# Layer ends in column form with weights as the stationary operand, and the second layer's end done once for all four batches

## The chip, the cores and the metric

The kernel runs on one core of a Trainium2 chip. The metric is device time in microseconds (us) of one execution. Executions of one kernel spread by 1 to 2% here, so medians and intervals are given; profiles are single executions. A run is called slow when it is over 1.5% above the fastest of its kernel in the same rounds, and fast otherwise; ratios use fast runs alone. Engines: PE multiplies matrices (PEld is its weight load), DVE is VectorE, ACT is ScalarE, POOL is GpSimd, SP issues the DMAs.

## The reference, cut to what matters

```
# A: attention block, B: gated block; 4 batches, one token each, D=512
# 32 query heads, 8 K/V heads, 4096 positions of 128; F=1792
x = x + A(layernorm(x))      # q = x@wq, softmax(q k^T / sqrt(128)) v, then @ wo
x = x + B(layernorm(x))      # (sigmoid(x@w_gate) * (x@w_up)) @ w_down
x = x + A(layernorm(x))      # the same weights and the same K/V cache
x = x + B(layernorm(x))
```

Below, "layer 1" and "layer 2" are the two passes through A and B. The "end" of a layer is everything after the attention values: output projection with `wo`, residual, layernorm, gate, up, down, residual. K is read once (both layers use it while it is in memory); V is read twice.

## The kernel before

The program keeps a list of operations with names of what they read and write; a small scheduler, working with assumed durations, fixes the order of each engine in advance. A PSUM bank is one name, so two operations that use one bank are ordered by the program's text, whatever their priority. K and V come through a ring of 22 slots of 512 KB. K tiles hold 16 slots from their load until layer 2's scores of that batch.

The ends of both layers are in row form: activations are the stationary operand (one column), weights stream past as the moving operand, and four matmuls work on four column groups of 32.

```
    def y_proj(s, oi, prio, gis=range(4)):            # output projection
        for gi in gis:
            for h in range(16 * s + gi * R, 16 * s + gi * R + R):
                for j in range(4):
                    mm(G_ps[32*j:32*j+1, 0:P], oT[oi][:, h:h+1], wo[:, h, j*P:(j+1)*P], h == 0, h == H-1)
            S.put("pe", ..., writes=["G"])
    def glu(x, xkey, o, okey, prio, last):
        layer_norm(x, xkey, xT[:], "xT", prio, True)   # rows; a matmul turns them into columns
        # gate into G_ps, up into U_ps: 16 matmuls each, 448 moving columns
        # tanh and multiply on 128x448, 5 small matmuls to columns, copy, 56 matmuls for down into G_ps
    ...
    for b in range(B):
        ...                                            # values and y_proj of layer 1
        cross(0, b, 0, PX)                             # end of layer 1, priority 0 (first)
        ...                                            # q projection and scores of layer 2
        if b > 0:
            for s in range(NH):
                y_proj(s, 1, PC)                       # end of layer 2 of the batch before,
            cross(1, b - 1, 1, PC)                     # priority 4 (last)
```

Of the kernel before, what the change touches and what calls it, by code (L numbers as in the profile page):

```python
# [12 lines left out]
RATE = 0.419  # L13
# [184 lines left out]
def bass_interleave_layers__gqa_block_cached__glu_gated_glu__decode_kernel(nc, A_x, A_k, A_v, A_wq, A_wo, B_x, B_wg, B_wu, B_wd, out):  # L198
# [3 lines left out]
    R = H // G  # L202
# [33 lines left out]
    wd = sb("wd", [P, 4, 3, D], bf)  # L236
    wd_r = sb("wd_r", [P, 2, D], bf)

    xin = [sb(f"xin{b}", [P, P], bf) for b in range(B)]
    xs = [sb(f"xs{i}", [P, P]) for i in range(2)]  # L240
    xc = sb("xc", [P, P], bf)
    cols = sb("cols", [P, 32])
    xsum = cols[:, 0:2]
    nmean, vpe, mhalf, rs_h = (cols[:, i:i + 1] for i in range(2, 6))
    rs_q = [[cols[:, 6 + 4 * l + b:7 + 4 * l + b] for b in range(B)] for l in range(2)]
    rows, nrows, ones, nbias = (cols[:, i:i + 1] for i in range(14, 18))
    ls = cols[:, 18:20]
    nM = cols[:, 20:20 + R]
    xT = sb("xT", [P, KD], bf)
    xT1 = sb("xT1", [P, KD, B], bf)  # L250
# [7 lines left out]
    th = sb("th", [P, FS])  # L258
    junk = th[:, FS - P:FS]
    h_sb = th[:, 0:FS // 2].bitcast(bf)  # L260
    hT = sb("hT", [P, 14], bf)
    oT = [sb(f"oT{i}", [P, H], bf) for i in range(2)]
# [17 lines left out]
    U_ps = ps("U_ps", [P, 512])  # L280

    sel4 = ident_b[:].rearrange("p (j y) -> p j y", y=32)[:, :, 0]
# [9 lines left out]
    sem_names += [f"wo{i}" for i in range(4)] + ["wg", "wu", "wd", "wd_r0", "wd_r1"]  # L292
    sem_names += [f"x{b}" for b in range(B)] + [f"out{b}" for b in range(B)]
# [11 lines left out]
    for name, t in (("ident_b", ident_b), ("rows", rows), ("nrows", nrows), ("mask_a", mask_a), ("sel_den", sel_den)):  # L305
        S.put("pool", lambda e, t=t: e.memset(t[:], 0.0), 0.15, 0, writes=[name])
    S.put("pool", lambda e: e.memset(mhalf[:], -0.5), 0.1, 0, writes=["mhalf"])
    S.put("pool", lambda e: e.memset(ones[:], 1.0), 0.1, 0, writes=["ones"])
    S.put("pool", affine(ident_b, ident_b[:], [[-1, P]], 0, 1.0), 0.3, 0, reads=["ident_b"], writes=["ident_b"])
    for j in range(4):  # L310
        S.put("pool", affine(rows, rows[:], [[0, 1]], -32 * j, 1.0 / D), 0.2, 0, reads=["rows"], writes=["rows"])
        S.put("pool", affine(nrows, nrows[:], [[0, 1]], -32 * j, -1.0 / D), 0.2, 0, reads=["nrows"], writes=["nrows"])
# [6 lines left out]
    for b in range(B):  # L319
        S.put("dve", lambda e, b=b: e.memset(xin[b][:], 0.0), 0.1, 0, writes=[f"xin{b}"])  # L320
    for b in range(B):
        S.put(
            "act", lambda e, b=b: e.dma_start(
                xin[b][bass.ds(0, 4, step=32), :], A_x[b, 0, :].rearrange("(j p) -> j p", j=4)
            ), 0.3, 0, writes=[f"xin{b}"], dma=f"x{b}",
        )
    for name, t, v in (("ml", ml, 1.0), ("mt", mt, 0.0), ("S0", S_ps[0], 0.0), ("S1", S_ps[1], 0.0), ("S2", S_ps[2], 0.0), ("G", G_ps, 0.0), ("U", U_ps, 0.0)):
        S.put("dve", lambda e, t=t, v=v: e.memset(t[:], v), 0.4, 0, writes=[name])
# [39 lines left out]
    def load_wd():  # L368
        src = B_wd.rearrange("(j f) n -> j f n", j=4)
        load_w(  # L370
            "wd", wd[:].rearrange("p j c n -> p j (c n)"),
            src[:, 0:FM, :].rearrange("j (p c) n -> p j (c n)", c=3), P * 12 * D * 2,
        )
        for i in range(2):
            load_w(
                f"wd_r{i}", wd_r[i * FR:(i + 1) * FR],
                src[2 * i:2 * i + 2, FM:FS, :].rearrange("j p n -> p j n"), FR * 2 * D * 2,
            )
# [30 lines left out]
    def stat(bank, key, c, src, si, w, wkey, prio):  # L409
        S.put(  # L410
            "pe", mm(bank[:, c:c + 1], col(w), xsum[:, si:si + 1]), 0.4, prio,
            reads=[f"xsum{si}", wkey], writes=[key],
        )

    def layer_norm(x, xkey, xT_ap, xT_key, prio, summed):
        if not summed:
            S.put(
                "dve", lambda e: e.tensor_scalar(junk, x[:], 1.0, None, op0=ALU.mult, op1=ALU.add, accum_out=xsum[:, 0:1]),  # L418
                0.35, prio, reads=[xkey], writes=["th", "xsum0"],
            )  # L420
        stat(U_ps, "U", 448, xsum, 0, nrows, "nrows", prio)
        S.put(
            "dve", lambda e: e.tensor_scalar(xc[:], x[:], U_ps[:, 448:449], None, op0=ALU.add), 0.3, prio,
            reads=[xkey, "U"], writes=["xc"],
        )
        S.put("dve", lambda e: e.tensor_copy(nmean[:], U_ps[:, 448:449]), 0.15, prio, reads=["U"], writes=["nmean"])  # L426
        S.put(
            "act", lambda e: e.activation(junk, x[:], ACTF.Square, bias=nmean[:], accum_out=xsum[:, 1:2]), 0.6, prio,  # L428
            reads=[xkey, "nmean"], writes=["th", "xsum1"],
        )  # L430
        S.put("pe", mm(U_ps[:, 452:456], xc[:], sel4), 0.25, prio, reads=["xc", "ident_b"], writes=["U"])
        S.put("dve", lambda e: e.tensor_copy(xT_ap, U_ps[:, 452:456]), 0.18, prio, reads=["U"], writes=[xT_key])  # L432

    def rstd(mult, rs, rs_key, prio, bank, key, c):
        stat(bank, key, c, xsum, 1, rows, "rows", prio)
        S.put(
            "dve", lambda e: e.tensor_scalar(vpe[:], bank[:, c:c + 1], mult, mult * eps, op0=ALU.mult, op1=ALU.add),  # L437
            0.17, prio, reads=[key], writes=["vpe"],
        )
        S.put(  # L440
            "pool", lambda e: e.tensor_tensor(rs[:], vpe[:], mhalf[:], ALU.pow), 0.6, prio,  # L441
            reads=["vpe", "mhalf"], writes=[rs_key],
        )

    def q_proj(s, xT_of, n, dst, dkey, prio, xkey):
# [8 lines left out]
        S.put("pe", fns, 2.4, prio, reads=[xkey, f"wq{2 * s}", f"wq{2 * s + 1}"], writes=["M"])  # L454
# [27 lines left out]
    def scores(b, s, u, prio):  # L482
        for q in range(2):
            fns = []
            bank, bkey = S_ps[(2 * u + q) % 3], f"S{(2 * u + q) % 3}"
            for nn in range(NQ):
# [11 lines left out]
                "pe", fns, 1.6, prio, reads=[f"qbd{u % NQB}"] + [f"kT{b}{4 * s + gi}{q}" for gi in range(4)],  # L498
# [3 lines left out]
    def softmax(u, rs, rs_key, prio):  # L502
# [3 lines left out]
        for q in range(2):  # L506
# [10 lines left out]
            "dve", lambda e: e.tensor_reduce(nM[:], tr[:, 0:16].rearrange("p (a h) -> p h a", h=R), AX.X, ALU.min),  # L517
# [4 lines left out]
                mt[:, 0:16].rearrange("p (a h) -> p a h", h=R), nM[:].unsqueeze(1).broadcast_to([P, 4, R])  # L522
# [4 lines left out]
            "dve", lambda e: e.tensor_scalar(nbias[:], nb[:, 0:1], rs[:], None, op0=ALU.mult), 0.22, prio,  # L527
            reads=["tr", rs_key], writes=["nbias"],
        )
        for q in range(2):  # L530
# [3 lines left out]
                    bias=nbias[:], scale=rs[:], accum_out=ls[:, q:q + 1],  # L534
                ), 0.85, prio, reads=[f"S{banks[q]}", "nbias", rs_key], writes=[f"p_sb{q}", f"ls{q}"],
# [18 lines left out]
        i0 = ls[:].unsqueeze(2).broadcast_to([P, 2, 16])  # L554
# [13 lines left out]
    def values(l, b, s, pi, oi, prio, gis=range(4)):  # L568
        for gi in gis:
            for q in range(2):  # L570
# [9 lines left out]
                S.put("pe", fns, 0.62, prio, reads=[f"pt{pi}"], writes=["O"], tiles=[tile])  # L580
        c0, c1 = gis[0] * R, (gis[-1] + 1) * R
        S.put(
            "dve", lambda e: e.tensor_tensor(  # L583
                oT[oi][:, 16 * s + c0:16 * s + c1], O_ps[:, c0:c1], winv[pi][:, c0:c1], ALU.mult
            ), 0.2, prio - 1.5, reads=["O", f"winv{pi}"], writes=[f"oT{oi}{s}{gi}" for gi in gis],
        )

    def y_proj(s, oi, prio, gis=range(4)):
        for gi in gis:
            fns = []  # L590
            for h in range(16 * s + gi * R, 16 * s + gi * R + R):
                for j in range(4):
                    fns.append(mm(
                        G_ps[32 * j:32 * j + 1, 0:P], oT[oi][:, h:h + 1], wo[:, h, j * P:(j + 1) * P], h == 0, h == H - 1,
                    ))
            S.put("pe", fns, 0.5, prio, reads=[f"oT{oi}{s}{gi}", f"wo{2 * s + gi // 2}"], writes=["G"])

    def glu(x, xkey, o, okey, prio, last):
        layer_norm(x, xkey, xT[:], "xT", prio, True)
        for w, key, bank, bkey in ((wg, "wg", G_ps, "G"), (wu, "wu", U_ps, "U")):  # L600
            fns = []
            for k in range(KD):
                for j in range(4):
                    fns.append(mm(
                        bank[32 * j:32 * j + 1, 0:FS], xT[:, k:k + 1], w[:, k, j * FS:(j + 1) * FS], k == 0, k == KD - 1,
                    ))
            S.put("pe", fns, 1.1, prio, reads=["xT", key], writes=[bkey])
            if w is wg:
                rstd(4.0, rs_h, "rs_h", prio, G_ps, "G", 448)
        S.put(  # L610
# [92 lines left out]
    for b in range(B):  # L703
        if b > 0:
            values(1, b - 1, 0, pis[1, b - 1, 0], 1, PV, range(pre))
# [70 lines left out]
```

## Time and profile before

The median was 368.5 us. The profiled execution has a span of 369.9 us.

| what | value |
|---|---|
| read from HBM | 114.6 MB |
| PE, PEld, DVE busy | 69%, 49%, 41% |
| unhindered DMA | about 410 GB/s, so some 280 us for the bytes |

From the page of the kernel before: busy time of the engines, then the span in 40 slices (a digit is the busy share in tenths) and the rate of the DMA in GB/s by slice.

```profile
PE 255.4 (69%) x5752; PEld 180.1 (49%) x5752; DVE 152.2 (41%) x396; ACT 61.2 (17%) x147; POOL 14.2 (4%) x56
DMA  8999999997599999972999979854999989727800
GB/s 276 400 397 410 399 350 401 407 340 291 174 410 409 408 364 332 357 287 73 328 411 408 396 267 357 284 220 152 384 400 410 364 282 359 288 105 240 334 4 3
```

The holes (174, 73, 152, 105 GB/s) are where the ring is full and the queue waits; each comes at the change from layer 1 to layer 2 of a batch. The last 20 us move nothing.

By stages, cut where the q projection of layer 2 begins in each batch (88.8, 164.6, 243.6 and 324.2 us). Columns: stretch, its length, busy time of each engine with the number of instructions, granted clock of PE (the share of its full clock that it was given), DMA share, GB/s.

```profile
0.00:88.80 88.80, 42.15 (x793) 29.45 (x794) 33.96 (x90) 10.97 (x28) 8.17 (x45) 0.69 1.02 377
88.80:164.60 75.80, 54.80 (x1245) 38.53 (x1243) 34.32 (x81) 13.27 (x31) 1.09 (x2) 0.55 0.90 339
164.60:243.60 79.00, 60.74 (x1407) 42.96 (x1405) 36.28 (x90) 14.40 (x34) 1.64 (x3) 0.56 0.84 311
243.60:324.20 80.60, 61.82 (x1408) 43.18 (x1406) 36.22 (x90) 14.40 (x34) 1.64 (x3) 0.54 0.84 317
```

The second and third period contain a whole layer-2 end of the batch before, the first only half of a projection. In all three the DMA share is well under 1.

Single steps, from the timeline (start, duration, engine and operation, number of instructions, and in brackets the idle time before and what ended it; "issue" means that the profile shows nothing that the engine waited for). Most lines between these are left out:

```profile
19.23 1.85 PE L297 MATMUL M_ps<-xT,wq 128*128 128x4 bf16 x64
208.54 0.17 DVE L583 TENSOR_TENSOR oT<-O_ps,winv 128x12 bf16<-128x12 f32 x1
221.48 1.66 PE L297 MATMUL G_ps<-wo,oT 128*1 128x128 bf16 x54
224.48 2.19 PE L297 MATMUL G_ps<-wo,oT 128*1 128x128 bf16 x74 [1.34 <-issue]
243.45 1.84 PE L297 MATMUL M_ps<-xT,wq 128*128 128x1 bf16 x64
342.20 1.66 PE L297 MATMUL G_ps<-wg,xT 128*1 128x448 bf16 x16 [0.76 <-DVE xT L432]
356.82 3.58 PE L297 MATMUL G_ps<-wo,oT 128*1 128x128 bf16 x128
362.15 0.93 PE L297 MATMUL G_ps<-wg,xT 128*1 128x448 bf16 x16 [0.26 <-DVE xT L432]
```

Three things are to be seen. The q projection (weights stationary) takes 1.84 us for 64 matmuls whether PE was granted full clock (at 19 us) or half (at 243 us). The gate, 448 moving columns, takes 0.93 us at full clock and 1.66 at half. And at 221 us the projection of layer 1 runs as one lump of 128, because its bank G was held by layer 2's end: the first of the values that it multiplies are ready at 208.7 us (the DVE line), and the last read of G by layer 2's end is over at 220.7. In the next period the same happens (ready at 289.0, bank free at 300.4, start at 301.7).

### The profile page before, as it was taken

The page shows a single profiled execution, that of the slowest core. Times are in us where ns is not written, and L with a number is a line of the kernel's source. Part 1 is how long each engine was busy: PE and PEld are TensorE (multiplying, and loading weights), DVE is VectorE, ACT ScalarE, POOL GpSimd, SP SyncE. Part 2 cuts the span into 40 slices and gives each one's busy share as a digit, 9 for nine tenths or more (in the row PEclk, how much of TensorE's full clock was granted, in tenths as well). Part 3 has the DMA queues.
Part 4 walks back from the last instruction along what each step waited for, and adds up shares of the span by engine and source line. Part 5 has one row for each costly group of instructions (what it writes and reads, how often), then busy time and mean ns, then how long its engine had stood idle before and what let it go on. Part 6 is the DMA issues. An engine that isn't in the chain of part 4 may idle for free.

```text
span 369.9 us, 12694 instructions
## 1 busy us (share of the span) xinstructions
PE 255.4 (69%) x5752; PEld 180.1 (49%) x5752; DVE 152.2 (41%) x396; ACT 61.2 (17%) x147; POOL 14.2 (4%) x56
## 2 busy tenths in 40 slices
PE   1361771666865775879475896978657977977994
PEld 1230641525342574565343675664424665763792
DVE  4939330021599611113898211115896311106112
ACT  1103011010142030100503210001421300103301
POOL 6100000000000000000000000000000000000000
PEclk9996555565765555556955555556555565556558
DMA  8999999997599999972999979854999989727800
GB/s 276 400 397 410 399 350 401 407 340 291 174 410 409 408 364 332 357 287 73 328 411 408 396 267 357 284 220 152 384 400 410 364 282 359 288 105 240 334 4 3
DMA packets 35911, 115.40 MB, mean 312 GB/s; under 512 B 3344, under 2 KB 7696, under 8 KB 35856
## 3 DMA queue, kind: packets, MB, share of 16 engines
q1 hardware_dynamic: 35792, 114.57, 82.8%
q8 instruction: 45, 0.74, 0.8%
q14 instruction: 10, 0.08, 0.1%
q10 hardware_dynamic: 64, 0.01, 0.0%
HBM read 114.56 MB, written 0.00 MB: 310 GB/s over the span
## 4 chain that ended last, share of the span: by engine, by line
PE 40%; DMA 34%; DVE 11%; SPq 7%; issue 6%; ACT 1%; POOLq 0%; DVEq 0%; ACTq 0%
DMA ring<-in_A_v_cache_dram 27%; PE G_ps L297 13%; PE O_ps L575 8%; PE S_ps L492 7%; PE M_ps L297 6%; SPq L339 5%; PE U_ps L297 4%; DMA wd_r<-in_B_w_down_dram 4%; DMA ring<-in_A_k_cache_dram 4%; DVE ring L479 3%; SPq L355 3%; DVE ml L508 2%; PE PT_ps L297 2%; DVE tr L515 1%; DVE tr L525 1%
## 5 line engine op out<-in xcount | busy, mean ns | idle before, releaser
L575 PE MATMUL O_ps<-pt_sb,ring 128*128 128x4 bf16 x2048 | 67.2, 167 | 32.5 <-DMA ring<-in_A_v_cache_dram 25.0
L575 PEld LDWEIGHTS O_ps<-pt_sb,ring 128*128 128x128 bf16 x2048 | 62.0, 105 | 49.4 <-issue 25.8
L479 DVE STREAM_TRANSPOSE ring<-ring 128x1024 int32<-128x1024 int32 x64 | 75.9, 1217 | 7.8 <-DMA ring<-in_A_k_cache_dram 7.7
L492 PE MATMUL S_ps<-ring,qbd 128*16 128x512 bf16 x512 | 54.5, 576 | 3.4 <-issue 1.6
L297 PE MATMUL G_ps<-wo,oT 128*1 128x128 bf16 x1024 | 33.0, 307 | 10.8 <-issue 8.9
L532 ACT ACTIVATE p_sb<-S_ps,cols 128x512 bf16<-128x512 f32 x32 | 24.6, 772 | 87.0 <-DVE cols L527 78.1
L508 DVE TENSOR_REDUCE ml<-S_ps 128x1 f32<-128x512 f32 x32 | 21.5, 673 | 32.2 <-PE S_ps L492 32.2
L297 PEld LDWEIGHTS G_ps<-wo,oT 128*1 128x1 bf16 x1024 | 25.0, 116 | 13.5 <-issue 10.7
L297 PE MATMUL PT_ps<-ident_b,p_sb 128*128 128x64 bf16 x128 | 11.1, 230 | 26.0 <-ACT p_sb L532 25.9
L492 PEld LDWEIGHTS S_ps<-ring,qbd 128*16 128x16 bf16 x512 | 13.7, 111 | 24.8 <-issue 19.4
L297 PEld LDWEIGHTS PT_ps<-ident_b,p_sb 128*128 128x128 bf16 x128 | 7.0, 117 | 33.9 <-ACT p_sb L532 32.3
L297 PE MATMUL M_ps<-dsel,cols 128*128 128x16 f32 x64 | 15.9, 366 | 9.2 <-DVE qbd L470 7.8
L583 DVE TENSOR_TENSOR oT<-O_ps,winv 128x12 bf16<-128x12 f32 (+2 forms) x29 | 4.7, 162 | 42.5 <-PE O_ps L575 41.8
L297 PE MATMUL U_ps<-cols 128*128 128x1 f32 x48 | 13.1, 342 | 13.1 <-POOL sel_den L300 6.4
L441 POOL TENSOR_TENSOR cols<-cols 128x1 f32<-128x1 f32 x16 | 8.8, 548 | 346.6 <-DVE cols L437 161.1
L428 ACT ACTIVATE th<-xs,cols 128x128 f32<-128x128 f32 x12 | 4.8, 401 | 99.5 <-DVE cols L426 99.5
L297 PEld LDWEIGHTS M_ps<-xT,wq 128*128 128x128 bf16 x640 | 18.8, 106 | 1.3 <-issue 0.7
L297 PEld LDWEIGHTS M_ps<-dsel,cols 128*128 128x128 f32 x64 | 14.3, 307 | 10.4 <-DVE qbd L470 8.4
L297 PEld LDWEIGHTS U_ps<-cols 128*128 128x128 f32 x48 | 11.2, 290 | 16.1 <-DVE th L418 6.4
L297 PE MATMUL M_ps<-xT,wq 128*128 128x1 bf16 (+1 forms) x640 | 18.6, 165 | 0.6 <-DVE qbd L470 0.6
L297 PE MATMUL G_ps<-wg,xT 128*1 128x448 bf16 x128 | 12.6, 540 | 1.3 <-DVE xT L432 1.3
L470 DVE TENSOR_TENSOR qbd<-M_ps,mask_a 128x256 bf16<-128x256 f32 x16 | 6.7, 418 | 15.8 <-PE M_ps L297 15.8
(74 smaller groups left out, 184.6 us busy)
## 6 DMA issues: line engine op xcount, KB each, us to landing
ring<-in_A_v_cache_dram SPq DMA_DIRECT2D x128, 512.0 KB, 7.8
ring<-in_A_k_cache_dram SPq DMA_DIRECT2D x64, 512.0 KB, 11.2
wq<-in_A_wq_dram SPq DMA_DIRECT2D x4, 1024.0 KB, 11.9
wo<-in_A_wo_dram SPq DMA_DIRECT2D x4, 1024.0 KB, 12.0
wg<-in_B_w_gate_dram SPq DMA_DIRECT2D x1, 1792.0 KB, 13.5
wu<-in_B_w_up_dram SPq DMA_DIRECT2D x1, 1792.0 KB, 11.1
wd<-in_B_w_down_dram SPq DMA_DIRECT2D x1, 1536.0 KB, 15.8
wd_r<-in_B_w_down_dram SPq DMA_DIRECT2D x2, 128.0 KB, 15.0
```

The lines of the kernel that those rows point to most:

```text
L297: return lambda e: e.matmul(o, lhsT=l, rhs=r, start=start, stop=stop)
L339: return e.dma_start(ring[t.slot], t.src.rearrange("(p t) d -> p (t d)", p=P)[:, q * TS:(q + 1) * TS])
L355: S.put("sp", lambda e: e.dma_start(o, i), 0.55, 0, writes=[key], dma=key, nbytes=nbytes)
L428: "act", lambda e: e.activation(junk, x[:], ACTF.Square, bias=nmean[:], accum_out=xsum[:, 1:2]), 0.6, prio,
L441: "pool", lambda e: e.tensor_tensor(rs[:], vpe[:], mhalf[:], ALU.pow), 0.6, prio,
L470: "dve", lambda e: e.tensor_tensor(dst, i0, i1, ALU.mult), 0.45, prio, reads=["M", "mask_a"],
L479: return e.transpose(v, v)
L492: return e.matmul(bank[32 * gi:32 * gi + 16, :], lhsT=qbd[u % NQB][:, gi, nn, :], rhs=kt[:, :, nn // 2, :, nn % 2], start=nn == 0, stop=nn ...
L508: "dve", lambda e, q=q: e.tensor_reduce(ml[:, q:q + 1], S_ps[banks[q]][:], AX.X, ALU.max, negate=True), 0.65,
L532: "act", lambda e, q=q: e.activation(p_sb[:, 4 * q:4 * q + 4, :].rearrange("p c x -> p (c x)"), S_ps[banks[q]][:], ACTF.Exp, bias=nbias[:] ...
L575: return e.matmul(O_ps[:, gi * R:(gi + 1) * R], lhsT=ring[tile.slot][:, (t % HT) * DH:(t % HT + 1) * DH], rhs=pt_sb[pi][:, t % 4, t // 4, ...
L583: "dve", lambda e: e.tensor_tensor(oT[oi][:, 16 * s + c0:16 * s + c1], O_ps[:, c0:c1], winv[pi][:, c0:c1], ALU.mult), 0.2, prio - 1.5, rea ...
```

## The change

Its intent is to drop the steps that turn rows into columns, and to do layer 2's end once, with four columns per matmul, instead of four times with one. Its core, with cuts:

```diff
-RATE = 0.419
+RATE = 0.409
...
-                        G_ps[32 * j:32 * j + 1, 0:P], oT[oi][:, h:h + 1], wo[:, h, j * P:(j + 1) * P], h == 0, h == H - 1,
+                    r = oT1[:, h:h + 1] if l == 0 else oT2[:, h, :]
+                        Y_ps[:, 0:nb * KD].rearrange("p (b k) -> p b k", b=nb)[:, :, j], wo[:, h, j * P:(j + 1) * P], r,
+                        h == 0 and j == 0, h == H - 1 and j == KD - 1,
...
-            for k in range(KD):
-                for j in range(4):
-                        bank[32 * j:32 * j + 1, 0:FS], xT[:, k:k + 1], w[:, k, j * FS:(j + 1) * FS], k == 0, k == KD - 1,
+            for f in range(NF):
+                for k in range(KD):
+                        dst[:, f * nb:(f + 1) * nb], w[:, k, f * P:(f + 1) * P], xk(k), k == 0, k == KD - 1,
...
-        fns = [mm(G_ps[:, 452 + 4 * c:456 + 4 * c], h_sb[:, bass.ds(c, P, step=3)], sel4) for c in range(3)]
-        S.put("dve", lambda e: e.tensor_copy(hT[:], G_ps[:, 452:466]), 0.2, prio, reads=["G"], writes=["hT"])
...
-        if b > 0:
-            for s in range(NH):
-                y_proj(s, 1, PC)
-            cross(1, b - 1, 1, PC)
...
+            values(1, B - 1, s, pis[1, B - 1, s], PV, gis)
+            y_proj(1, s, PX, gis)
+    cross(1, None, PX)
```

The layernorms at the start are also done once for four batches, the down weights are loaded in one piece, and some durations that the scheduler assumes were set anew.

## The prediction

> **What bounds the kernel.** The span is 369.9 us; 114.6 MB come from HBM. Unhindered slices show about 410 GB/s, so the bytes need some 280 us. PE is busy 69%, DVE 41%. The kernel alternates: full DMA, then stretches where the 22-slot ring is full until PE frees slots. The slices show five holes (174, 73, 152, 105, then 4 and 3 GB/s). By stage windows, a batch period takes 76 us (89–165), 79 (165–244), 80 (244–324) for about 25 MB (61 us at 410 GB/s). About 10 us of it is the hole between the end of layer 1 and the first layer-2 scores (164–174, 246–255, 327–335: DMA near 0); the rest are stretches at 0.66–0.85 DMA share where PE is saturated and runs the previous batch's layer-2 end (212–220, 292–300). From 345 to 360 PE is 100% busy; DMA is done by 350.
>
> **What changes, costed.**
> - Per matmul little is won. 64 weight-stationary matmuls (q projection) took 1.84 us, 28 ns each, at granted clock 1.00 and 0.50 alike. The old output projection took 3.6 us per 128: the same. Gate (or up) took 1.66 us at clock 0.5, 0.93 at 1.0; the new 56 matmuls should take 1.6 at either. Down: 1.9 (1.1 at full clock) becomes 1.6. The Trainium skill ("TensorE: Matmul & The Clock Gate", fast weight load) gives it to full 128-column non-fp32 weights; the trace agrees: they stream at 28 ns.
> - Removed: three of four layer-2 ends: each about 3.6 us output projection, 1.66+0.6+1.66 gate/stat/up, 0.4 transposes, 1.9 down, 0.6 stat: 10 us of PE, 30 in all.
> - Shortened: each layer-1 end. Tanh 0.64 and multiply 0.62 on 128x448 become about 0.2 each; transposes plus copy (0.75 with waits) and two layernorm transposes plus copies (0.35 each) go. About 3 us of chain per batch.
> - Layer-1 output projections no longer wait for a PSUM bank the layer-2 end holds (221–227, one 4 us lump); the final one can interleave with values (357–360 today).
> - Added: DVE steps for four batches and a transpose at the very end; the chain after the projection should stay near 9.5 us (360.5–369.9 before), as gate and up lose the full-clock advantage.
>
> **On the critical path.** Layer-1 chains: 1 us in batch 0 (down weights landing at 84.3 end the wait there), 3 in each of three batches: 10. Layer-2 ends out of two middle periods: 3.5 each, as the first period without one is that much shorter: 7. Output projections removed or unlumped: 5. Tail: layer-2 end of batch 2 (6 us while PE is saturated) and the exposed last projection (3): 8.5, limited by the last values' landing. Sum about 30 us; the rest of the removed PE time falls under DMA-bound stretches.
>
> **Predicted:** 338 us, range 328 to 350. Chances: faster by over 2% 0.95, within 2% 0.04, slower 0.01.
>
> **What would show it.** PE busy falls by about 30 us; gate and up have 56 matmuls in 1.5–1.8 us whatever the clock; middle periods 70–72 us; holes of 6–8 us; last DMA landing near 325–330 and 10–13 us from it to the end. The start (0–84) unchanged, at DMA share 0.98 or more.
>
> **What would make it wrong.** K tiles hold slots until layer-2 scores, so holes could stay; DVE transposes of K (saturated in 104–124) may take over; PE's unexplained "issue" gaps (1–2 us) may persist. In the other direction the retuned static order could close more low-share stretches than I assume.

## The result, and the profile after

The kernel after has a median of 347.9 us (346.5 to 348.8, 4 runs) against 368.3 (366.7 to 371.9, 4 runs): the ratio is 0.943, with a 95% interval of 0.935 to 0.951. A ratio here is the mean time of one kernel's fast runs over that of the other's fast runs of the same rounds, so it isn't quite the ratio of the medians. That is 20 us faster; 30 had been predicted, and 347.9 is near the upper end of the range that was given.

The page of the kernel after, the same lines:

```profile
PE 222.9 (65%) x5426; PEld 171.2 (50%) x5426; DVE 138.4 (40%) x341; ACT 52.8 (15%) x128; POOL 10.6 (3%) x38
DMA  7999999999489999998599999957999999977800
GB/s 264 375 401 409 408 345 365 409 401 377 192 275 405 410 407 372 374 381 320 172 393 409 409 368 347 404 179 280 334 416 407 410 354 382 343 284 256 356 5 2
```

PE lost 32.5 us of busy time, yet its weight loads still take half of the span. The Trainium skill ("Perfetto Trace Analysis", Identifying the Most-Contended Engine) advises judging PE by the arithmetic that it gets done and by the share of weight loads, rather than by the busy share of matmuls; here the share of weight loads went from 49% to 50% while that of matmuls fell from 69% to 65%, and the holes in the DMA became fewer and shallower but are still there.

The stages after, cut at the same events, with the tail in two pieces:

```profile
0.00:87.70 87.70, 36.08 (x844) 27.70 (x845) 30.30 (x68) 8.04 (x18) 5.79 (x30) 1.00 1.00 376
87.70:156.90 69.20, 51.61 (x1250) 39.15 (x1251) 32.62 (x77) 12.71 (x31) 1.09 (x2) 0.62 0.92 351
156.90:229.80 72.90, 51.42 (x1248) 39.17 (x1248) 32.80 (x78) 12.72 (x31) 1.08 (x2) 0.52 0.89 336
229.80:301.80 72.00, 52.36 (x1251) 39.82 (x1250) 32.92 (x79) 12.71 (x31) 1.08 (x2) 0.52 0.95 362
301.80:327.00 25.20, 19.66 (x481) 14.44 (x482) 7.24 (x26) 6.41 (x16) 0.55 (x1) 0.64 0.81 297
327.00:344.20 17.20, 11.75 (x364) 10.97 (x361) 2.51 (x14) 0.25 (x1) 1.01 (x1) 0.50 0.01 4
```

The periods of 75.8, 79.0 and 80.6 us became 69.2, 72.9 and 72.0: 21 us less. The tail, from the q projection of the last batch to the end, went from 45.7 us (369.9 less 324.2; 45.9 from the exact start, as in the table below) to 42.4, only 3.3 less. The start lost 1.1 us. This sums to 25.7 us, more than the 20 us between the medians: the profiled run of before was 3.4 us above its median and that of after 1.4 us below. Stage by stage the single profiles are thus good to a few us, no better.

What held up the projection of layer 1 is gone. In period 2 of after it starts when its first values are ready, and runs in four pieces, of which the first and the last are:

```profile
201.84 1.44 PE L298 MATMUL Y_ps<-oT,wo 128*128 128x1 bf16 x48 [0.70 <-DVE oT L580]
214.01 0.58 PE L298 MATMUL Y_ps<-oT,wo 128*128 128x1 bf16 x16 [0.26 <-DVE oT L580]
```

Counted from the start of its period, this projection ends at 57.7 us in both periods 2 and 3 of after; in before it ended at 62.2 and 64.0. So 4.5 and 6.3 of the 6.0 and 8.6 us that these periods lost lie before the end of the projection, and 1.6 and 2.4 in the chain from there to the q projection.

The end of the tail after (timeline, PE alone, some lines left out near the end):

```profile
323.81 1.45 PE L298 MATMUL Y_ps<-oT,wo 128*128 128x4 bf16 x48 [0.35 <-DVE oT L580]
325.12 0.99 PE L571 MATMUL O_ps<-pt_sb,ring 128*128 128x4 bf16 x32
326.38 0.59 PE L298 MATMUL Y_ps<-oT,wo 128*128 128x4 bf16 x16 [0.26 <-DVE oT L580]
326.83 0.43 PE L571 MATMUL O_ps<-pt_sb,ring 128*128 128x4 bf16 x11
327.90 2.43 PE L571 MATMUL O_ps<-pt_sb,ring 128*128 128x4 bf16 x85 [0.64 <-issue]
330.68 1.52 PE L298 MATMUL Y_ps<-oT,wo 128*128 128x4 bf16 x48 [0.35 <-DVE oT L580]
333.31 0.59 PE L298 MATMUL Y_ps<-oT,wo 128*128 128x4 bf16 x16 [0.26 <-DVE oT L580]
335.43 1.65 PE L298 MATMUL G_ps<-xTj,wg 128*128 128x4 bf16 x56 [0.47 <-DVE xTj L411]
```

From 318 us on PE works nearly without a break: values and projection take turns, with short waits for DVE to empty the one bank of values. The gate takes 1.65 us, close to 56 times 28 ns.

### The profile page after: what moved, and what is told of

It is laid out like the page before. It is cut to its first block, busy times and chain, and to the rows that moved or that the text cites. A ratio compares the mean times of both kernels' runs of the same rounds, so it can differ in the third digit from the quotient of the medians.

```text
span 344.2 us, 11881 instructions
## 1 busy us (share of the span) xinstructions
PE 222.9 (65%) x5426; PEld 171.2 (50%) x5426; DVE 138.4 (40%) x341; ACT 52.8 (15%) x128; POOL 10.6 (3%) x38
## 4 chain that ended last, share of the span: by engine, by line
DMA 40%; PE 27%; issue 14%; DVE 10%; SPq 7%; POOLq 0%; ACT 0%; DVEq 0%
DMA ring<-in_A_v_cache_dram 31%; PE S_ps L488 7%; PE O_ps L571 6%; PE M_ps L298 6%; PE Y_ps L298 5%; DMA wd<-in_B_w_down_dram 5%; SPq L331 5%; DVE ring L475 4%; DMA wo<-in_A_wo_dram 3%; PE G_ps L298 2%; SPq L347 2%; DVE ml L504 2%; DMA ring<-in_A_k_cache_dram 2%; PE PT_ps L298 1%; DVE qbd L466 1%
## 5 line engine op out<-in xcount | busy, mean ns | idle before, releaser
L571 PEld LDWEIGHTS O_ps<-pt_sb,ring 128*128 128x128 bf16 x2048 | 63.7, 105 | 48.0 <-DMA ring<-in_A_v_cache_dram 20.3
L475 DVE STREAM_TRANSPOSE ring<-ring 128x1024 int32<-128x1024 int32 x64 | 75.8, 1216 | 8.6 <-DMA ring<-in_A_k_cache_dram 8.2
L298 PE MATMUL Y_ps<-oT,wo 128*128 128x1 bf16 (+1 forms) x640 | 20.4, 166 | 9.2 <-DVE oT L580 5.7
L298 PEld LDWEIGHTS Y_ps<-oT,wo 128*128 128x128 bf16 x640 | 18.7, 104 | 11.5 <-DVE oT L580 7.0
L298 PE MATMUL M_ps<-xT,wq 128*128 128x1 bf16 x512 | 15.4, 165 | 6.7 <-issue 4.1
L298 PEld LDWEIGHTS M_ps<-xT,wq 128*128 128x128 bf16 x512 | 14.5, 104 | 7.5 <-issue 4.3
L437 POOL TENSOR_TENSOR cols<-cols 128x1 f32<-128x1 f32 (+1 forms) x10 | 6.4, 640 | 325.0 <-issue 217.4
L298 PEld LDWEIGHTS M_ps<-dsel,cols 128*128 128x128 f32 x64 | 13.7, 298 | 3.4 <-DVE dsel L553 2.8
L426 ACT ACTIVATE gs<-xj,cols 128x4 f32<-128x4 f32 x8 | 2.4, 297 | 81.6 <-DVE cols L424 81.6
L547 ACT ACTIVATE pt_sb<-PT_ps 128x512 bf16<-128x512 f32 x16 | 9.6, 597 | 22.4 <-PE PT_ps L298 22.4
L298 PE MATMUL G_ps<-cols 128*128 128x1 f32 (+1 forms) x40 | 11.4, 354 | 2.4 <-DVE cols L403 0.9
L536 ACT ACTIVATE p_sb<-PT_ps 128x512 bf16<-128x512 f32 x16 | 9.6, 597 | 12.3 <-PE PT_ps L298 12.3
## 6 DMA issues: line engine op xcount, KB each, us to landing
wd<-in_B_w_down_dram SPq DMA_DIRECT2D x1, 1792.0 KB, 16.4
```

The lines of the kernel that those rows point to most:

```text
L298: return lambda e: e.matmul(o, lhsT=l, rhs=r, start=start, stop=stop)
L437: "pool", lambda e: e.tensor_tensor(rs, vpe[:, 0:nb], mhalf[:, 0:nb], ALU.pow), 0.6, prio,
L475: return e.transpose(v, v)
L536: "act", lambda e: e.activation(pt1.rearrange("p c g a h -> p (c g a h)"), PT_ps[:], ACTF.Copy), 0.65, prio,
L547: "act", lambda e: e.activation(pt_sb[pi][:].rearrange("p q c g h -> p (q c g h)"), PT_ps[:], ACTF.Copy), 0.65,
L571: return e.matmul(O_ps[:, gi * R:(gi + 1) * R], lhsT=ring[tile.slot][:, (t % HT) * DH:(t % HT + 1) * DH], rhs=pt_sb[pi][:, t % 4, t // 4, ...
```

## The experiments

All stage lengths below are read from the timeline as above: from the start to the first q projection of layer 2, the three periods, the tail.

| kernel | median us | start | period 1 | period 2 | period 3 | tail |
|---|---|---|---|---|---|---|
| before | 368.3 to 370.3 | 88.7 | 75.8 | 79.0 | 80.6 | 45.9 |
| after | 347.9 | 87.7 | 69.2 | 73.0 | 72.0 | 42.4 |
| ends per batch, first try (e1) | 375.4 | 87.5 | 69.6 | 83.1 | 82.1 | 50.4 |
| ends per batch, mended (e7) | 366.7 (fast runs) | 87.4 | 68.3 | 80.5 | 79.3 | 50.7 |
| after, with PE dummies (e5) | 354.5 | 87.1 | 68.8 | 74.7 | 72.7 | 48.9 |
| after, layer-1 projection in a lump (e8) | 353.3 | 87.5 | 69.6 | 77.1 | 75.7 | 42.6 |
| after, last projection late (e4) | 347.9 | 87.7 | 69.2 | 74.6 | 73.6 | 42.6 |

Up to the tail, e4's program does the same work in the same way as after's, and its periods 2 and 3 still read 1.6 us longer: differences of that size mean nothing here.

The first theory was that the once-only end was worth about half of the gain, through PE time, and column form the other half. The rivals gave all to the one or to the other.

### e1: the second layer's end per batch again, in column form

```diff
+        if b > 0:
+            for s in range(NH):
+                y_proj(1, s, PC, b=b - 1)     # one column, oT2[:, h, b:b+1]
+            cross(1, b - 1, PC)
...
+            S.put("pe", mm(M_ps[0:KD, 320:448], xo[:], ident_b[:]), ..., writes=["M"])   # result to rows
```

> The changed kernel with one part undone: the second layer ends for each batch by itself again (one column per matmul, four times), where the kernel before had it; column form is kept. Before 368.3, after 348.0. Theory: the once-only end is worth about half of the gain, as PE time taken out of stretches where PE is saturated, and column form the other half: 357 to 361 us. Rival A, all the gain is column form and the removed PE time lay under DMA: 348 to 351. Rival B, column form gives nothing and all is the once-only end: 365 to 369.

It took 375.4 us (374.5 to 377.8), ratio 1.015 to before: outside all that was expected. The trace showed a flaw of the experiment. The new transposing of the result used bank M, and the matmul for the softmax denominators of the next attention, which came later in the program's text, had to wait for it; values waited in turn, and the DMA stood at 0 to 1 GB/s from 208 to 214 us. This run is no verdict on the question, but it showed what a bank shared with a low-priority job can do, which led to e5 and e8.

### e7: the same, with the transposing through bank G

```diff
-            S.put("pe", mm(M_ps[0:KD, 320:448], xo[:], ident_b[:]), ..., writes=["M"])
+            S.put("pe", mm(G_ps[0:KD, 320:448], xo[:], ident_b[:]), ..., writes=["G"])
```

> The run with per-batch ends again, with its flaw mended: there the transposing of the result shared the M bank with the softmax denominators, which kept the next values waiting (DMA stood still from 208 to 216 us). Now it goes through the G bank. Before 368 to 370, after 348, dummies (PE time alone) 354.5. If column form alone is worth about half of the gain: 357 to 361. If the once-only end is nearly all: 364 to 370. If the per-batch ends cost no more than their PE time: 354 to 356.

One of its four runs, 369.5 us, is slow; the fast ones took 363.9, 366.7 and 368.1, ratio 0.991 (0.983 to 0.999) to before, which counts as the same at the limit of 2%. So column form alone gives about 1%, if anything, and the once-only end the other 19 us (366.7 less 347.9, from different rounds). The stages of this run:

```profile
87.40:155.80 68.40, 52.00 (x1249) 39.53 (x1250) 32.67 (x78) 12.71 (x31) 1.08 (x2) 0.52 0.93 355
155.80:236.20 80.40, 59.15 (x1550) 47.62 (x1549) 34.10 (x86) 13.15 (x34) 1.62 (x3) 0.56 0.86 314
236.20:315.60 79.40, 60.57 (x1553) 48.17 (x1551) 34.14 (x87) 13.15 (x34) 1.62 (x3) 0.52 0.87 321
315.60:366.30 50.70, 37.98 (x1141) 32.94 (x1140) 10.03 (x44) 7.61 (x22) 1.62 (x3) 0.60 0.41 149
```

Column form does shorten period 1, which holds no whole layer-2 end, by 7.5 us. In periods 2 and 3 nothing of it is left beside layer 2's ends (80.4 and 79.4 against 79.0 and 80.6), and the tail is 4.8 us longer than before. The tail now runs 1141 matmuls where before ran 923, and PE waits more for its instructions (see e6). Sums of PE's pauses of over 0.25 us that the profile names issue, in us:

| kernel | period 2 | period 3 | tail |
|---|---|---|---|
| before | 4.0 | 6.1 | 2.2 |
| after | 5.0 | 4.6 | 2.3 |
| e7 | 10.2 | 10.7 | 6.2 |
| e5 (below) | 8.2 | 6.5 | 5.5 |

In the tail e7 pauses 4.1 us longer than before, of the 4.8 that it lost. In periods 2 and 3 it pauses 11.3 us longer than after. Two steps of it, the lump of layer 1's projection and a pause among the last values that it still needs:

```profile
216.54 3.12 PE L300 MATMUL Y_ps<-oT,wo 128*128 128x1 bf16 x112
222.60 0.28 PE L573 MATMUL O_ps<-pt_sb,ring 128*128 128x4 bf16 x5 [2.65 <-issue]
```

So two things hold up e7 there, the bank and the instructions, and no run separates them. Between before and after the pauses are the same in sum (10.1 and 9.6 us in both periods), so they don't explain that difference.

### e5: the PE time of the removed ends, without their waits

```diff
+        if b > 0:
+            for i in range(18):   # 288 matmuls that nobody reads
+                fns = [mm(G_ps[:, 256:257], wo[:, (i + n) % H, 0:P], ident_b[:, 0:1]) for n in range(16)]
+                S.put("pe", fns, 0.55, PC, reads=["ident_b", "wo3"], writes=["G"])
```

> The changed kernel plus 288 matmuls per batch (three times, about 8 us of PE each) that nobody reads, at the priority and place of the second layer's ends, with no waits on VectorE or ScalarE results of their own. If what counted in the once-only end is PE occupancy, the time is within 2 us of the run with per-batch ends (theory: 356 to 360). If it was the chain of small steps and the shared PSUM bank, the dummies cost little: 348 to 351.

It took 354.5 us (353.2 to 355.0), 6.6 more than after and 12.1 less than e7's fast runs. The stages:

```profile
155.90:230.60 74.70, 59.30 (x1537) 46.77 (x1538) 33.02 (x78) 12.71 (x31) 1.08 (x2) 0.55 0.90 340
230.60:303.20 72.60, 60.02 (x1537) 47.19 (x1536) 33.04 (x78) 12.71 (x31) 1.08 (x2) 0.52 0.92 348
303.20:352.10 48.90, 39.20 (x1130) 33.49 (x1127) 9.80 (x41) 6.54 (x17) 1.55 (x2) 0.53 0.41 151
```

PE is as busy in periods 2 and 3 (59.3 and 60.0 us) as in e7 (59.2 and 60.6), yet these periods are only 1.7 and 0.7 us longer than after's, where e7's are 7.5 and 7.3 longer. The 1.7 and 0.7 us are no more than what two profiles of the same code differ by (e4). PE time that can run whenever PE is free fits into the gaps. In the tail the same matmuls, some 8 us of PE, with 3.2 us of longer pauses cost 6.4 us: there PE has few gaps. So the first theory falls for the middle and holds for the tail.

### e8: only the lump

```diff
-                y_proj(0, s, PX, gis)
+                if b < 2:
+                    y_proj(0, s, PX, gis)
+        if b >= 2:
+            for s in range(NH):
+                y_proj(0, s, PX, more=["oT013"])   # waits for the last value
```

> The changed kernel, but in batches 2 and 3 the first layer's output projection waits for all of its values and runs as one lump of 128 matmuls, as it had to in the kernel before while the second layer's end held its PSUM bank. Theory: the bank that the second layer's end held, not its PE time, cost the middle periods: the lump adds about 3 us per period, 353 to 355. Rival, the lump is hidden under the wait for values: 348 to 350.

It took 353.3 us (350.7 to 354.8), 5.4 more than after, as expected. The stages:

```profile
157.20:234.20 77.00, 51.97 (x1248) 39.43 (x1248) 33.01 (x78) 12.71 (x31) 1.08 (x2) 0.52 0.89 325
234.20:309.90 75.70, 51.82 (x1250) 39.18 (x1248) 32.83 (x79) 12.71 (x31) 1.08 (x2) 0.55 0.91 342
```

With no more PE work than after, periods 2 and 3 are 4.1 and 3.7 us longer. The chain from the last value to the q projection, during which K keeps its slots, became longer by most of a lump: 128 matmuls (3.6 us) now follow the last value, where in after 16 do (0.6 us). Pauses for instructions are also longer here, 13.1 us in the two periods against 9.6. This run imitates what the bank does to the projection; a run in which the second layer's end has a bank of its own, which would show it directly, was not made.

### e4: the last projection after all values

```diff
-            y_proj(1, s, PX, gis)
+    for s in range(NH):
+        y_proj(1, s, 6)          # lowest priority
```

> The changed kernel with the second layer's output projection (128 matmuls, 3.6 us) put after all values, as the kernel before had it at its end, instead of between them. My prediction counted 3 us for the interleaving. Theory now: from 318 to 334 us PE is saturated, so interleaving hides nothing: time within 1 us of the changed kernel's (347 to 349). Rival, as predicted: 351, 3 us more.

It took 347.9 us (345.6 to 350.0), the same as after. (The scheduler still put 32 of the 128 matmuls into gaps; 96 ran as a lump.) Where PE is saturated, interleaving hides nothing.

### e6: the program shifted by 64 matmuls

```diff
+    S.put("pe", [mm(G_ps[:, 256:257], ident_b[:], ident_b[:, 0:1]) for _ in range(64)], 1.8, PX, ...)
```

> The changed kernel with 64 matmuls that nobody reads put at the very start, where PE is idle. Theory: PE's gaps of 1.5 to 2.9 us that the profile names issue come from fetching PE's instructions in blocks of 16 KB (128 matmuls with their weight loads), so they move 64 matmuls earlier in the program: the one inside the gate matmuls (46 before it, 10 after) and the one inside the spreading of q (7 before, 9 after) leave these places. Time within 2 us of 348. Rival, the gaps belong to the work they fall in (a wait that the profile does not show): they stay at the same matmuls.

It took 349.6 us (348.4 to 351.0), 1.7 more than after, less than the spread. Two timelines of PE around the same work, first after, then the shifted one:

```profile
219.86 1.36 PE L298 MATMUL G_ps<-xT,wg 128*128 128x1 bf16 x46
224.08 0.42 PE L298 MATMUL G_ps<-xT,wg 128*128 128x1 bf16 x10 [2.85 <-issue]
...
234.80 0.24 PE L298 MATMUL M_ps<-q2T,ident_b 128*32 128x16 bf16 x9 [2.54 <-issue]
```

```profile
219.95 1.63 PE L298 MATMUL G_ps<-xT,wg 128*128 128x1 bf16 x56
221.44 0.56 PE L298 MATMUL G_ps<-cols 128*128 128x1 f32 x2
221.87 1.53 PE L571 MATMUL O_ps<-pt_sb,ring 128*128 128x4 bf16 x52
224.82 0.46 PE L571 MATMUL O_ps<-pt_sb,ring 128*128 128x4 bf16 x12 [1.43 <-issue]
...
231.34 1.60 PE L298 MATMUL M_ps<-xT,wq 128*128 128x1 bf16 x54 [2.45 <-issue]
...
237.24 0.38 PE L298 MATMUL M_ps<-xT,wq 128*128 128x1 bf16 x9 [1.49 <-issue]
```

The pauses left the gate and the spreading of q, as expected. The one in the spreading had 7 of 16 matmuls before it; 64 matmuls earlier (7, two statistics, 55 of the 64 of the q projection) is where the new one stands, within one matmul. In the shifted run consecutive pauses are 12+56+32+2+16+10 = 128 and 54+2+16+55 = 127 matmuls apart. So the pauses belong to a place in PE's instruction stream, not to the work. The page's table of DMA queues counts, on the queue of kind "instruction" that carries most, 42 packets with 0.69 MB for after: 16 KB each. 5426 matmuls and as many weight loads over 42 packets are 258 instructions a packet; for before (5752 and 45 packets) 256, for e7 (6329 and 49) 258. PE's instructions thus arrive in blocks of about 128 matmuls. The trace times these packets too: each of the nine pauses of over 0.25 us in after ends 1.3 to 1.5 us after one of them has landed. PE eats a block in 3.6 us when it runs without a break, and then it can wait for the next, 0.3 to 2.9 us in after and 14.1 us in all nine. Most of the pauses fall where the DMA is full, but not all: during the last one above (1.49 us) the DMA moved 11 GB/s, and during one of 2.16 us in before (at 326.9 us) 2 GB/s. So a full DMA is not what makes them.

### e2 and e3: the scheduler's numbers alone

e2 is after with before's queue rate and durations, e3 is before with after's.

```diff
-RATE = 0.409
+RATE = 0.419
-            S.put("pe", fns, 2.0, prio, reads=[xkey, ...
+            S.put("pe", fns, 2.4, prio, reads=[xkey, ...
```

> The changed kernel with the old numbers for the static schedule (queue rate 0.419, old durations of q projection, scores, exponentials and values). If the retuned model gave some of the gain: 351 or more. Theory: under 2 us, 346 to 350.

> The kernel before with the new numbers for the static schedule alone. Theory: within 1.5% of before (363 to 373). If the retuning were a main cause: 360 or less.

e2 took 348.8 us (347.3 to 349.0). e3 took 370.0 in its three fast runs (367.2 to 370.7; ratio 0.999); the fourth, 374.9, is slow, and its profile fell in it. The retuning is no cause.

### e9, e10, e11: attempts at a better version that failed

e9 gives the ring a 23rd slot, paid for by three instead of four buffers of probabilities. e10 adds, in the tail, a second PSUM bank for values. e11 adds the down weights in one contiguous piece per partition.

```diff
-    NS = 22                                              # e9
+    NS = 23
-    NPT = 4
+    NPT = 3
+            free = (2 * cnt["u"]) % 3                    # e10: a bank of scores is free by then
+            values(1, B - 1, s, pis[1, B - 1, s], PV, gis, None if len(gis) == 3 else (S_ps[free], f"S{free}"))
-B_wd.rearrange("(c p) n -> p c n", p=P)                  # e11
+B_wd.rearrange("(p c) n -> p c n", p=P)
-                        dst[:, f * nb:(f + 1) * nb], w[:, k, f * P:(f + 1) * P], xk(k), k == 0, k == KD - 1,
+                        dst[:, f * nb:(f + 1) * nb], w[:, k, bass.ds(f, P, step=NF)], xk(k), k == 0, k == KD - 1,
```

> The changed kernel with 23 ring slots instead of 22 and three buffers of probabilities instead of four (the memory that this frees, with what the change freed, is one slot). What still stops the DMA is that the ring is full until the second layer's scores free the K tiles: each more slot is 0.5 MB, about 1.3 us of transfer at 410 GB/s, in each of three middle holes. Theory: 343 to 346 us, if the three buffers are enough; if they are not, or the holes are set by PE, 347 to 350.

> As the run with 23 slots, and in the tail the last values of each half go to a free PSUM bank, so that PE need not wait for VectorE to empty the one bank before each output projection (four waits of 0.26 to 0.35 us between 323 and 334 us). Theory: 1 us less than the run with 23 slots.

> As the run before, and the down weights are loaded with 14 KB per partition in one piece instead of 14 rows of 1 KB, with gate and up weights read with a stride of 14 columns to match. Theory: the load lands up to 0.8 us earlier in batch 0 where its landing ends the wait; against that, if strided weight loads take longer than 28 ns, up to 1.6 us more for each 56 matmuls: between 1 us faster and 10 us slower, the profile's duration of 56 gate matmuls tells which.

e9 took 390.2 us: its periods are 84, 85 and 88 us. By the program's text four probability buffers are alive at a time (two halves of two layers); with three, each period loses 12 to 16 us. That the buffers are the reason is argued, since the slot was changed with them; the extra slot cannot be judged. e10 took 388.6, 1.6 less than e9, about as expected, though the intervals overlap. e11 took 395.5, 7 us more than e10, for a reason that its timeline shows:

```profile
383.36 3.48 PE L298 MATMUL Y_ps<-xTj,wu 128*128 128x4 bf16 x56
387.22 1.66 PE L298 MATMUL Y_ps<-hT,wd 128*128 128x4 bf16 x56 [0.38 <-DVE hT L648]
```

56 matmuls whose weights are read with a step of 14 columns take 3.48 us, 62 ns each; the packed ones after them 1.66. The down weights landed 16.4 us after issue as in the kernel after.

### e12: a version meant to beat both

```diff
-    pre = 3
+    pre = 2                                    # V tiles of the batch before, ahead of the next K
-    PX, PS, PV, PC, PK = 0, 2, 2.2, 4, 2.1
+    PX, PS, PV, PC, PK = 0, 2, 2.2, 4, 3       # K transposes behind scores and values
+            ... the second bank of e10
```

> A version meant to beat both, with 22 slots and four buffers of probabilities again: the second PSUM bank for the last values of the tail, which took 1.6 us off the run with 23 slots; two instead of three heads' values of the batch before loaded ahead of the next K tiles; and the transposes of K put below the values and scores in the order of VectorE. Theory: the tail is 1 to 2 us shorter and the middle periods 1 us each: 343 to 346 us. If the order is worth nothing: 346 to 347.

Its five fast runs took 340.9 to 344.7 us, median 343.7 (the sixth, 346.2, is slow), ratio 0.931 (0.927 to 0.935) to before, so it beats before. The kernel after was not run in the same rounds; against its median the gain is 4.3 us, about 1%, and its own ratio of 0.943 has an interval that begins (0.935) where e12's ends. That it beats after is likely, not shown. Its profile fell in a slow run, so it isn't used for stages, and which of the three edits did it is not separated.

## Why the prediction was right or wrong

The direction was right and the time lies in the range, but the gain was 20 us where 30 were predicted.

**PE time: right.** "PE busy falls by about 30 us": 32.5. "Gate and up have 56 matmuls in 1.5–1.8 us whatever the clock": 1.63 to 1.65. The Trainium skill ("TensorE: Matmul & The Clock Gate", Back-to-back issue gap) gives about 60 cycles, an issue floor of some 25 ns, for up to 64 moving columns at full clock; the trace has 28 to 29 ns a matmul (3.57 us for 128 in e8, 1.84 for 64), and, which the section doesn't say, the same at half clock.

**Middle periods: the sum nearly right, its parts not.** "Middle periods 70–72 us" became 73.0 and 72.0. The prediction priced the layer-2 ends by their PE time (7 us) and gave 5 to the unlumped projections. e5 shows that PE time alone is worth no more than 1.7 and 0.7 us there; e8 shows that the lump alone is worth 4.1 and 3.7 us (5.4 in total by the medians). In the kernel before, the first part of layer 1's projection stood ready 11 to 12 us before its bank came free, and 10.8 of the 14.6 us that the two periods lost lie before the end of that projection. So what layer 2's end cost in the middle was mostly that it kept layer 1 waiting, and the bank is what the trace shows it waiting for. e7 loses 14.8 us to after in these periods; PE time and the lump make up about 10 of them by e5 and e8, but e7's longer pauses for instructions (11.3 us) overlap with both, and no run separates them.

**"Layer-1 chains ... 3 in each of three batches": mis-sized both ways.** In period 1 column form took 7.5 us off (e7). From the end of the projection to the q projection it is 13.7 us there (142.1 to 155.8) against 19.4 (145.1 to 164.5) before. But before's chain also contained 64 matmuls of layer 2's projection (1.8 us), and pauses for instructions of 2.2 us (2.0 in e7). Without these it is 15.3 us against 11.7, so 3.7 us are column form's own, not far from the 3 predicted. In periods 2 and 3 the same chain is 1.6 and 2.4 us shorter in after than in before, hardly more than the 64 matmuls that left it, so there the predicted 3 us didn't come. The two parts of the change are not additive: alone, column form is worth about 1%.

**Tail: the step that failed.** "Tail: layer-2 end of batch 2 ... and the exposed last projection (3): 8.5" measured 3.3 to 3.5. Interleaving the last projection is worth nothing (e4), since PE is saturated. Between the first probabilities of the last batch being ready and the end of the projection the time fell from 18.3 us (342.1 to 360.4) to 15.4 (318.5 to 333.9), not by the 6 us of removed PE work: four waits of 0.26 to 0.35 us for DVE and a pause of 0.64 us took some of it back. And the chain after the projection grew from 9.5 us (360.4 to 369.9) to 10.3 (333.9 to 344.2): gate and up gave up their full-clock speed of 0.93 us, and the power operation on four columns takes 1.01 us on POOL instead of 0.55. "10–13 us" from the last DMA to the end became 17. The removed end is still worth having there: e7, which puts it back in column form, has a tail 8.3 us longer than after's, with 4.0 us more of pauses.

**Its other marks.** The start was to stay unchanged at a DMA share of 0.98: it has 1.00, and is 1.0 us shorter. Holes were to be 6 to 8 us: by the packets of the trace, the ring's queue stood still for 5.1, 7.1, 7.1 and 7.6 us at the four changes from layer 1 to layer 2 of before, and for 4.2, 3.4, 1.1 and 2.6 in after. Pauses named issue were to stay, and did (16.8 us before, 14.1 after).

**The remaining 5 us** between the sum of the stages (25.7) and the medians (20.4) are spread between executions; which stage varies, single profiles don't tell.

## What to carry to other kernels

Before a removed piece of work is priced by its engine time, ask what it holds while it runs: here a low-priority job that owned a PSUM bank delayed a high-priority one, and by e5 and e8 that cost more than its matmuls, which would have fitted into gaps. Interleaving work into an engine that is saturated hides nothing, so count the tail by the engine's total there. And a form with more and smaller matmuls is paid for in instructions as well: at 28 ns each, PE can run ahead of the delivery of its own program (e7 paused for 29.1 us in all, after for 14.1).

## What the Trainium skill lacked or had wrong

- "Runtime: NRT & Kernel Launch", Instruction fetch mechanics, tells that instructions come by DMA in blocks of 16 KiB, 256 instructions each, and calls the cost of crossing a block boundary mostly hidden. The blocks are as it says (42 packets of 16 KB for 10852 instructions, pauses 127 to 128 matmuls apart in e6). The cost is not hidden here: nine pauses of 0.3 to 2.9 us in after, 14.1 us in sum, and 29.1 us in e7.
- "TensorE: Matmul & The Clock Gate", Weight-path perf modes, allows column steps up to 1,024 elements for fast weight load and gives no price: with a step of 14, a matmul with its weights took 62 ns instead of 29 (3.48 against 1.63 us for 56, e11 and after). Whether the load was a fast one there, the trace doesn't say.
- The same page, Back-to-back issue gap, gives cold and warm formulas by moving columns alone. It says that weight loads set the spacing too, but for streams of weight load and matmul it has figures for 128 and 512 moving columns only. A stream of 128-column weights with 1 or 4 moving columns took 29 ns each at granted clock 0.50 and 1.00 alike (1.84 and 1.85 us for 64).
